# Three more feed-forward steps with P-Q+N on VectorE, and one batch load moved by two steps

## The chip, the core and the metric

The kernel runs on one core of a Trainium2 chip. The core has TensorE (matmuls into PSUM, an accumulator memory), VectorE, ScalarE and GpSimd (elementwise work; GpSimd also issues DMAs) and SyncE (issues DMAs). The engines run side by side, each through its own instructions in order, and wait for each other at semaphores. The metric is device time in microseconds (us); every time below is in that unit unless it says ns. In the profile's lines PE is TensorE, PEld its weight load, DVE VectorE, ACT ScalarE, POOL GpSimd, SP SyncE; L872 is line 872 of the kernel before.

## What is computed

```python
def _attn_ref(x):                      # x: (8, 3008, 256)
    X = np.fft.fft(x, axis=1)
    X = np.fft.fft(X, axis=2)
    return X.real.astype(np.float32)

def _moe_ref(x, w_in, w_out):          # (24064, 256), (256, 2048), (2048, 256)
    h = np.maximum(x @ w_in, 0.0)
    return (h * h @ w_out).astype(np.float32)
```

The second function is applied to the rows of the first one's result. So: the real part of a two-dimensional Fourier transform of each of eight batches, then a feed-forward layer with a squared ReLU, in float16 products with float32 sums.

## The kernel before, in words

*Columns and blocks.* The real part of the transform of real data is symmetric, so the kernel computes only half of its frequencies, 1505 columns per batch, 12040 in all. They are cut into 25 blocks, numbered from 0 (`w` in the loop over `range(NW)`); the widths are 240, 512, 376, 376, 512, 448, then 512, and the last one 360. For each column it holds two vectors, `zc` (cosine part) and `zs` (sine part). The first feed-forward product of a column is P+Q, with P from `zc` and Q from `zs`; that of its mirror frequency is P-Q. One row of `zs` (the Nyquist row) must not change its sign in the mirror image; N is the term that mends it.

*Steps.* The 2048 hidden units are taken in eight steps of 256 (`s` from 0 to 7, `NST` is 8). A step fills one of two PSUM buffers `ph` (two chunks of 128 units) and makes both results from it:

- A plain step: `pq` multiplies for P+Q (L859, L860, two each), ScalarE takes the ReLU (L891), `turn` adds -2Q to the same PSUM (L882, two matmuls), ScalarE takes the ReLU again (L891). VectorE squares both in one instruction, the power (L898).
- A VectorE step, one listed in `diff[w]`: `cosines` multiplies for P alone (L868, two), VectorE forms 2P+N from it (`twice`, L872, PSUM and SBUF to SBUF), `sines` adds Q to the PSUM (L877, two matmuls, which must wait for L872), ScalarE takes the ReLU of P+Q (L891), and VectorE adds 2P+N to the negated P+Q and clips (L889, the custom operation), which gives the ReLU of P-Q+N. ScalarE squares the first half (`power_act`, L902), VectorE the second (L898, half as long). There is no L882. N for the step is a product `n2` of the spread Nyquist row `zn` and the weights, two GpSimd instructions (L818) into one of three buffers.

Between the matmuls of a step stand one eighth of the second feed-forward product of the block before (`f2s`, L704, 128x256 each, its results leave through L719 on ScalarE and L683 on SyncE's queue), and, in some steps, a share of the matmuls that make the next block's `zc` and `zs` (`zl`, L581). `lo` and `hi` are the steps from which and before which these are dealt out. Their results leave PSUM by L586 and L592 on ScalarE and, for mirrored columns, by L610 on VectorE; when the next step is a VectorE step, `held` keeps L610 back until `settle` of that step, after its L872 and the power of the step before. In the step `hi` the Nyquist row of the next block starts its way (`spread_nyq`: L809 on ScalarE's queue to DRAM, L810 on GpSimd's queue back into all partitions); `nyq_rows` then makes the next block's n in the steps that follow, and what is left of them in step 0 of that block.

When two VectorE steps follow each other, the L889 of the first (`pend`) is put behind the L872 of the second, and one group of four L704 of the next step (`f2s[s].pop(0)()`) is done ahead of that step's first matmul.

*Batches.* A batch is loaded by three DMAs on GpSimd's queue (`load_x`: L127 and two L132), into the one buffer `xo`, and folded by VectorE in steps that `put` and `late` place: for each batch there is a block `b0`, with the first folds (L431, L442) in `b0 - 1`, more (L435, L445, L460, L448) in `b0`, the late folds (L488, L499, in steps 3, 4 and 5) in `b0 + 1`. `b0` is 5, 8, 10, 13, 16 and 19 for the batches 2 to 7 in order; batch 4, whose `b0` is two after the one before, is the one that is `tight`. A block in `shared` has its step 4's second power on ScalarE (L902) in step 5 instead of on VectorE.

What is listed in `diff` before: (4, 6) in blocks 3 to 5, (1, 3, 5, 7) in 6 and 7, (1, 3) in 9, (1, 2, 4, 6, 7) in 11, and so on. The order of the work on each engine is the order in which the Python code records it; nothing reorders it.

Of the kernel before, what the change touches and what calls it, by code (L numbers as in the profile page):

```python
# [29 lines left out]
def kernel(  # L30
# [15 lines left out]
    B, S, D = x.shape  # L46
# [33 lines left out]
    NW = len(wins)  # L80

    def win_of(col):
        return max(w for w in range(NW) if wins[w][0] <= col) if col < TOT else NW
# [5 lines left out]
    col_of = {}  # L89
# [60 lines left out]
    def load_rows(i):  # L150

        b, t = bs[i], xs[i]
        o = b * S * D
        if b == 0:
            nc.gpsimd.dma_start(out=t[0:1, 0, R - 1, :], in_=bass.AP(tensor=x.tensor, offset=x.offset + o, ap=[[D, 1], [1, D]]))
        if b + 1 == B:
            nc.gpsimd.dma_start(
                out=t[1:2, 2, :, :].rearrange("p c d -> p (c d)"),
                in_=bass.AP(tensor=x.tensor, offset=x.offset + o + (S - R) * D, ap=[[XW, 1], [1, XW]]))
# [578 lines left out]
    def fold_jobs(i):  # L738
        f = folds[i] = fold_steps(i)
        return [f["d_even"], f["n_cos"], lambda: (f["d_odd"](), f["load"]()), f["n_sin"], f["odds"], f["nyq"], lambda: (f["even"](), f["away"]()), f["back"]]  # L740

    NST = NFC // 2
    at_of = {w: [[] for _ in range(NST)] for w in range(NW)}
    post_of = {w: [[] for _ in range(NST)] for w in range(NW)}
    diff = {w: (4, 6) if w < 6 else (1, 3, 5, 7) if w < NW - 4 else (1, 2, 4, 6, 7) for w in range(3, NW)}
    backs = []
    shared = []

    def put(w, s, i, name, *k, d=at_of):
        d[w][s].append(lambda: folds[i][name](*k))  # L750

    def late(w, s, i, *st):
        at_of[w][s].append(lambda: run(*[folds[i]["late"][k] for k in st]))

    def make(i):
        folds[i] = fold_steps(i)

    for i in range(2, B):
        b0 = (win_of(col_of[i, 0]) + win_of(col_of[i - 1, 1])) // 2 - 1
        tight = b0 - 2 in [(win_of(col_of[j, 0]) + win_of(col_of[j - 1, 1])) // 2 - 1 for j in range(2, i)]  # L760
        near = i == 2 or tight
        at_of[b0 - 1][0].append(lambda i=i: make(i))
        at_of[b0 - 2][7].append(lambda i=i: load_rows(i))
        backs.append(b0)
        late(b0 + 1, 3, i, 0)
        late(b0 + 1, 4, i, 1)
        for k in (2, 3, 4):
            late(b0 + 1, 5, i, k)
        put(b0 - 1, 5 if near else 3, i, "d_even", 0)
        put(b0 - 1, (6 if tight else 7) if near else 5, i, "d_even", 1)  # L770
        put(b0 if i == 2 else b0 - 1, 0 if i == 2 else 7 if near else 6, i, "n_cos")
        put(b0, 0, i, "d_odd", 0)
        put(b0, 1, i, "d_odd", 1)
        put(b0, 2, i, "n_sin")
        put(b0, 3, i, "even")
        put(b0, 4, i, "away")
        put(b0, 5, i, "odds")
        put(b0, 6, i, "back")
        put(b0, 6, i, "nyq", d=post_of)
        if i + 1 < B and b0 > 5 and (win_of(col_of[i + 1, 0]) + win_of(col_of[i, 1])) // 2 - 1 > b0 + 2:  # L780
            put(b0 + 1, 2, i, "load")
        else:
            put(b0, 7, i, "load")
        if b0 > 5:
            diff[b0] = (2, 4, 6)
            diff[b0 + 1] = (1, 2, 4, 6, 7)
            shared.append(b0 + 1)
        if tight:
            diff[b0 - 1] = (1, 3)
            shared.remove(b0 - 1)  # L790
    n2s = {}
    BIG = 3.0e38
# [28 lines left out]
    for w in range(NW):  # L821
# [4 lines left out]
        lo, hi = 0, NST - 4 if 1 in diff.get(w + 1, ()) else NST - 3 if w + 1 in diff else NST - 2  # L826
        at, post = at_of[w], post_of[w]
        if w == 1:
            fj = fold_jobs(1)
            at = [[], fj[0:1], fj[1:2], fj[2:3], fj[3:5], [], [], []]  # L830
            post[5] = fj[5:6]
        elif w == 2:
            te = table_steps(1)
            at = [[folds[1]["even"], folds[1]["away"]], [lambda: te["freq"](), lambda: te["args"](0)], [lambda: f0s["v_part"](0)], [lambda: f0s["v_part"](1), f0s["even"], f0s["away"], f0s["back"]],
                  [lambda: te["turns"](0)], [lambda: te["mods"](0)], [lambda: te["absm"](0), lambda: te["sins"](0)], [lambda: te["coss"](0)]]
        elif w == 3:
            at[0] = [lambda: te["weigh"]()]
            for st in range(5):
                at[1 + st // 3] = at[1 + st // 3] + f0s["late"][st : st + 1]
            at[3] = [folds[1]["back"]]  # L840
            lo, hi = 3, NST - 1
        elif w == win_of(col_of[1, 1]) - 1:
            for st in range(5):
                at[min(st, 3)] += folds[1]["late"][st : st + 1]
            lo, hi = 4, NST - 1
# [217 lines left out]
```

## Time and profile before

| | |
|---|---|
| runs | 598.60, 597.36, 598.44; median 598.44 |
| the profiled execution | 597.31, of which the span from the first to the last instruction is 595.5 |
| granted TensorE clock, mean | 0.999 |
| TensorE busy | 584.9 (98% of the span), 4421 matmuls |
| VectorE busy | 497.0 (83%), 582 instructions |
| ScalarE busy | 462.2 (78%), 617 instructions |
| GpSimd busy | 243.9 (41%), 304 instructions |
| DMA | 50.33 MB, 85 GB/s on the mean |

The busy times are unions: overlapping instructions of one engine count once. A matmul's length in the records reaches into the next one, since they are pipelined, so a busy TensorE can still lose time; what a matmul costs is read from the time between two starts. In a line of the timeline the first number is the start in us from the span's start, the second the length, then engine, line, operation, output and inputs, shapes and the number of instructions merged; in brackets, where there is one, the idle time of the engine before it and what ended it.

### The profile page before, as it was taken

The page shows a single profiled execution, that of the slowest core. Times are in us where ns is not written, and L with a number is a line of the kernel's source. Part 1 is how long each engine was busy: PE and PEld are TensorE (multiplying, and loading weights), DVE is VectorE, ACT ScalarE, POOL GpSimd, SP SyncE. Part 2 cuts the span into 40 slices and gives each one's busy share as a digit, 9 for nine tenths or more (in the row PEclk, how much of TensorE's full clock was granted, in tenths as well). Part 3 has the DMA queues.
Part 4 walks back from the last instruction along what each step waited for, and adds up shares of the span by engine and source line. Part 5 has one row for each costly group of instructions (what it writes and reads, how often), then busy time and mean ns, then how long its engine had stood idle before and what let it go on. Part 6 is the DMA issues. An engine that isn't in the chain of part 4 may idle for free.

```text
span 595.5 us, 11299 instructions
## 1 busy us (share of the span) xinstructions
PE 584.9 (98%) x4421; PEld 424.9 (71%) x4421; DVE 497.0 (83%) x582; ACT 462.2 (78%) x617; POOL 243.9 (41%) x304
## 2 busy tenths in 40 slices
PE   7999999999999999999999999999999999999997
PEld 4567786776776777777777777777777777777786
DVE  8988686987989778979899799979899799888871
ACT  6796777967797787788878788877877788788762
POOL 8411423166514506183253651446505724425310
PEclk9999999999999999999999999999999999999999
DMA  8946421137211461246123442145312321211212
GB/s 149 154 87 149 123 73 44 48 108 148 61 44 55 129 138 49 72 101 155 41 59 108 94 116 58 38 121 115 90 39 90 87 58 37 61 47 48 61 56 70
DMA packets 37624, 50.33 MB, mean 85 GB/s; under 512 B 4589, under 2 KB 30755, under 8 KB 37571
## 3 DMA queue, kind: packets, MB, share of 16 engines
q0 software_dynamic: 10400, 24.94, 20.6%
q1 hardware_dynamic: 26899, 24.44, 13.6%
q8 instruction: 34, 0.56, 0.4%
q10 hardware_dynamic: 272, 0.23, 0.1%
q14 instruction: 19, 0.16, 0.1%
HBM read 36.42 MB, written 27.86 MB: 108 GB/s over the span
## 4 chain that ended last, share of the span: by engine, by line
PE 81%; DVE 10%; ACT 3%; POOL 2%; issue 2%; DMA 1%; DVEq 0%; ACTq 0%; POOLq 0%
PE po L704 47%; PE ph L882 6%; PE ph L859 6%; PE ph L860 6%; PE ph L877 6%; PE ph L868 5%; PE pz L581 4%; DVE h L898 2%; DVE t L872 2%; DVE h L889 2%; DMA xo<-in_x_dram,idx_r 1%; ACT h L891 1%; DVE zc L610 1%; ACT h L902 1%; POOL xo L132 1%
## 5 line engine op out<-in xcount | busy, mean ns | idle before, releaser
L704 PE MATMUL po<-wout,h 128*128 128x256 f16 (+1 forms) x3024 | 364.8, 273 | 0.0
L704 PEld LDWEIGHTS <-h 128*128 128x128 f16 (+1 forms) x3024 | 296.8, 98 | 75.1
L891 ACT ACTIVATE h<-ph 128x1024 f16<-128x1024 f32 (+3 forms) x301 | 287.6, 991 | 64.2 <-PE ph L877 41.1
L898 DVE TENSOR_TENSOR h<-h 128x2048 f16<-128x2048 f16 (+7 forms) x199 | 189.9, 960 | 22.1 <-ACT h L891 18.9
L818 POOL TENSOR_SCALAR n<-zn,g2n 128x512 f32<-128x512 f16 (+3 forms) x166 | 156.2, 954 | 68.7 <-DMA zn<-rd 55.5
L872 DVE SCALAR_TENSOR_TENSOR t<-ph,n 128x1024 f32<-128x1024 f32 (+3 forms) x83 | 99.1, 1194 | 37.5 <-PE ph L868 32.1
L889 DVE CUSTOM_DVE_ANT_0 h<-t,ph 128x1024 f16<-128x1024 f32 x74 | 90.0, 1216 | 15.5 <-ACT h L891 15.1
L902 ACT ACTIVATE h<-h 128x1024 f16<-128x1024 f16 (+3 forms) x87 | 90.3, 1038 | 0.5
L719 ACT ACTIVATE osb<-po 128x512 f32<-128x512 f32 (+3 forms) x95 | 55.0, 584 | 37.0 <-PE po L704 32.5
L859 PE MATMUL ph<-zc,gh 128*128 128x512 f16 (+3 forms) x218 | 80.3, 369 | 0.4 <-ACT h L950 0.3
L860 PE MATMUL ph<-zs,gh 128*128 128x512 f16 (+3 forms) x218 | 80.2, 368 | 0.0
L810 POOL DMA_DIRECT2D zn<-rd x22 | 12.7, 579 | 161.9 <-DMA rd<-zs 153.6
L882 PE MATMUL ph<-zs,gh 128*128 128x512 f16 (+3 forms) x218 | 62.5, 368 | 0.3 <-ACT h L891 0.3
L877 PE MATMUL ph<-zs,gh 128*128 128x512 f16 (+3 forms) x166 | 48.4, 373 | 0.9 <-DVE t L872 0.4
L868 PE MATMUL ph<-zc,gh 128*128 128x512 f16 (+3 forms) x166 | 48.4, 373 | 0.0
L859 PEld LDWEIGHTS <-gh 128*128 128x128 f16 x218 | 21.2, 97 | 22.9 <-DVE h L889 1.6
L860 PEld LDWEIGHTS <-gh 128*128 128x128 f16 x218 | 21.3, 98 | 22.1 <-issue 0.9
L868 PEld LDWEIGHTS <-gh 128*128 128x128 f16 x166 | 16.2, 98 | 18.9 <-issue 0.5
L882 PEld LDWEIGHTS <-gh 128*128 128x128 f16 x218 | 20.2, 98 | 4.1 <-issue 0.7
L586 ACT ACTIVATE es<-pz 128x376 f32<-128x376 f32 (+1 forms) x32 | 14.8, 485 | 8.9 <-PE pz L581 8.7
L464 POOL DMA_DIRECT2D scr<-ev x8 | 4.7, 582 | 40.7 <-DVE ev L460 34.8
L132 POOL DMA_INDIRECT xo<-in_x_dram,idx_r x15 | 17.7, 1182 | 4.5 <-issue 4.3
(143 smaller groups left out, 368.2 us busy)
## 6 DMA issues: line engine op xcount, KB each, us to landing
out_dram<-osb SPq DMA_DIRECT2D x77, 128.0 KB
xo<-in_x_dram POOLq DMA_DIRECT2D x7, 768.0 KB, 6.8
scr<-ev POOLq DMA_DIRECT2D x8, 390.0 KB, 4.0
zn<-rd POOLq DMA_DIRECT2D x19, 128.0 KB, 3.9
rb<-scr POOLq DMA_DIRECT2D x16, 130.0 KB, 3.9
out_dram<-osb SPq DMA_DIRECT2D x12, 94.0 KB
w<-in_moe_w_in_dram POOLq DMA_DIRECT2D x2, 512.0 KB, 10.0
wout<-in_moe_w_out_dram POOLq DMA_DIRECT2D x1, 1024.0 KB, 11.0
```

Of the source, the lines that this page charges most:

```text
L704: nc.tensor.matmul(po[0:m, j * D : (j + 1) * D], h2[:, fc, q : q + m], wout16[:, fc, :], start=(fc == 0 and not both), stop=(fc == NFC - 1 ...
L818: nc.gpsimd.tensor_scalar(out=n2[:, a, 0:wn1], in0=zns[wt][:, 0:wn1], scalar1=g2n[:, fc : fc + 1], scalar2=1.0, op0=ALU.mult, op1=ALU.mult)
L859: nc.tensor.matmul(ph[:, a, 0:wn], gh[:, 0, f0 : f0 + P], zcw[:, 0:wn], start=True, stop=False)
L860: nc.tensor.matmul(ph[:, a, 0:wn], gh[:, 1, f0 : f0 + P], zsw[:, 0:wn], start=False, stop=True)
L868: nc.tensor.matmul(ph[:, a, 0:wn], gh[:, 0, f0 : f0 + P], zcw[:, 0:wn], start=True, stop=True)
L872: nc.vector.scalar_tensor_tensor(out=t2[:, :, 0:wn], in0=phs[s][:, :, 0:wn], scalar=-2.0, in1=n2s[w, s][:, :, 0:wn], op0=ALU.mult, op1=ALU ...
L877: nc.tensor.matmul(phs[s][:, a, 0:wn], gh[:, 1, f0 : f0 + P], zsw[:, 0:wn], start=False, stop=True, skip_group_check=True)
L882: nc.tensor.matmul(phs[s][:, a, 0:wn], gh[:, 2, f0 : f0 + P], zsw[:, 0:wn], start=False, stop=True, skip_group_check=True)
L889: nc.vector._custom_dve(TENSOR_ADD_SAT, out=h, in0=t2s[s][:, :, 0:wn], in1=phs[s][:, :, 0:wn], s0=BIG, s1=0.0)
L891: nc.scalar.activation(h, phs[s][:, :, 0:wn], AF.Relu, bias=0.0, scale=-1.0)
L898: nc.vector.tensor_tensor(h, h, h, op=ALU.mult)
L902: nc.scalar.activation(h, h, AF.Square, bias=0.0, scale=1.0)
```

## The change

```diff
@@ -742,9 +742,9 @@
-    diff = {w: (4, 6) if w < 6 else (1, 3, 5, 7) if w < NW - 4 else (1, 2, 4, 6, 7) for w in range(3, NW)}
+    diff = {w: (4, 6, 7) if w == 3 else (4, 6) if w < 6 else (1, 3, 5, 7) if 6 < w < NW - 4 else (1, 2, 4, 6, 7) for w in range(3, NW)}
     backs = []
-    shared = []
+    shared = [6]
@@ -777,7 +777,7 @@
-        if i + 1 < B and b0 > 5 and (win_of(col_of[i + 1, 0]) + win_of(col_of[i, 1])) // 2 - 1 > b0 + 2:
+        if i + 1 < B and (win_of(col_of[i + 1, 0]) + win_of(col_of[i, 1])) // 2 - 1 > b0 + 2:
             put(b0 + 1, 2, i, "load")
         else:
             put(b0, 7, i, "load")
@@ -786,7 +786,7 @@
         if tight:
-            diff[b0 - 1] = (1, 3)
+            diff[b0 - 1] = (1, 2, 4)
             shared.remove(b0 - 1)
@@ -838,7 +838,7 @@
             at[3] = [folds[1]["back"]]
-            lo, hi = 3, NST - 1
+            lo, hi = 3, NST - 2
         elif w == win_of(col_of[1, 1]) - 1:
```

In block 3 step 7 becomes a VectorE step, the matmuls for block 4's `zc` and `zs` are dealt to steps 3 to 5 instead of 3 to 6, and the Nyquist row of block 4 starts in step 6 instead of 7. In block 6 the VectorE steps 1, 3, 5, 7 become 1, 2, 4, 6, 7, and the second power of step 4 goes to ScalarE. In block 9 they go from 1, 3 to 1, 2, 4. The load of batch 3's data moves from step 7 of block 5 to step 2 of block 6. Everywhere else the order of instructions stays as it was.

In all that is three VectorE steps more: six L882 less on TensorE, three L872, three L889 and some halved powers on VectorE, three pairs of L818 more on GpSimd, one L902 more on ScalarE for step 4 of block 6 (in the new VectorE steps an L902 stands for the second L891). In blocks 3 and 6 the steps 6 and 7 now follow each other, in blocks 6 and 9 the steps 1 and 2, with the changed order of L889 and L704 that goes with it.

## The prediction

> **What bounds the kernel now.** I read the busy time by stretches first, one stretch per block (from its first L859 or L868 to the next block's). Columns: stretch, its length, then busy time and instructions of TensorE, weight loads, VectorE, ScalarE, GpSimd, then granted clock, DMA share and rate.
> ```profile
> 70.90:89.56 18.66, 18.66 (x162) 15.07 (x160) 14.67 (x26) 14.52 (x23) 5.77 (x8) 1.00 0.26 74
> 134.14:157.41 23.27, 23.11 (x166) 16.02 (x164) 18.75 (x25) 17.92 (x24) 12.60 (x17) 1.00 0.57 122
> 204.87:230.25 25.38, 25.38 (x185) 18.00 (x184) 19.17 (x26) 19.88 (x28) 6.66 (x9) 1.00 0.51 110
> 254.75:279.32 24.57, 24.57 (x184) 17.71 (x182) 19.97 (x26) 20.10 (x29) 13.37 (x17) 1.00 0.57 131
> ```
> These are blocks 3, 6, 9 and, for comparison, 11, which already has the five steps that block 6 gets. TensorE is busy nearly throughout, VectorE for 75 to 81%: a step costs its matmuls, plus waits. Second, the timeline, for the price of a step (start, length, what):
> ```profile
> 154.80 0.59 PE L868 MATMUL ph<-zc,gh 128*128 128x512 f16 x2
> 155.23 1.91 PE L704 MATMUL po<-wout,h 128*128 128x256 f16 x16
> 155.50 1.23 DVE L872 SCALAR_TENSOR_TENSOR t<-ph,n 128x1024 f32<-128x1024 f32 x1
> 156.98 0.59 PE L877 MATMUL ph<-zs,gh 128*128 128x512 f16 x2
> ...
> 180.03 1.22 DVE L872 SCALAR_TENSOR_TENSOR t<-ph,n 128x1024 f32<-128x1024 f32 x1
> 181.30 0.59 PE L877 MATMUL ph<-zs,gh 128*128 128x512 f16 x2 [0.38 <-DVE t L872]
> ```
> Two 512-column matmuls take 0.43 (154.80 to 155.23), sixteen L704 take 1.75, so twelve take 1.31. L872 starts 0.70 after L868, and L877 can start 1.27 after L872 (180.03 to 181.30, where it waited). So a VectorE step needs 0.70+1.27 = 1.97 between L868 and L877; TensorE gives 2.18 with sixteen L704 between them, only 1.74 with twelve. Summing what start-to-start times exceed these spacings: 0 in blocks 3 and 9, 0.48 in 6 (step 5: 0.18 before L868, 0.30 before L877), 0.55 in 7, 1.05 in 4. Third, the end of block 3:
> ```profile
> 85.06 0.48 PE L868 MATMUL ph<-zc,gh 128*128 128x376 f16 x2
> 85.38 1.47 PE L704 MATMUL po<-wout,h 128*128 128x256 f16 x12
> 85.43 0.83 ACT L891 ACTIVATE h<-ph 128x752 f16<-128x752 f32 x1
> 85.66 0.94 DVE L872 SCALAR_TENSOR_TENSOR t<-ph,n 128x752 f32<-128x752 f32 x1 [0.42 <-PE ph L868]
> 86.51 0.93 DVE L898 TENSOR_TENSOR h<-h 128x1504 f16<-128x1504 f16 x1
> 87.45 0.62 DVE L610 SCALAR_TENSOR_TENSOR zs<-es,pz 128x135 f16<-128x135 f32 x2
> 87.98 0.61 DVE L610 SCALAR_TENSOR_TENSOR zc<-es,pz 128x135 f16<-128x135 f32 x2
> 88.51 0.94 DVE L889 CUSTOM_DVE_ANT_1 h<-t,ph 128x752 f16<-128x752 f32 x1
> 89.56 0.38 PE L859 MATMUL ph<-zc,gh 128*128 128x512 f16 x1
> 92.08 0.59 PE L882 MATMUL ph<-zs,gh 128*128 128x512 f16 x2 [0.18 <-ACT h L891]
> ```
> Step 6: VectorE does L872, the power of step 5, four L610, then L889. Block 4's first L882 waits for ScalarE.
>
> **The change, part by part.**
>
> *Matmuls removed.* Three steps lose two L882 each: 2 x 0.43 (blocks 6, 9) + 0.32 (376 columns, 85.06 to 85.38) = 1.18 off.
>
> *Block 3: +1.16.* The z matmuls go from 5,5,5,5 in steps 3 to 6 to 6,7,7,0, so step 6's L868 starts 0.29 later (the time of its z, 86.69 to 86.98): 85.35, and L872 at 85.95. The power of step 5 needs that step's second L891 on ScalarE, and the two L592 copies now stand before it: L719 moves from 84.95 to 85.15, copies from 85.63, 0.38 each, L891 from 86.39 to 87.21. Power at 87.26, 0.94 to the next start; four L610, 0.53 a pair, to 89.26. Only there stands L872 of the new step 7: it ends at 90.20, L877 goes at 90.25. TensorE was ready at 85.35 + 0.32 + 1.31 + 0.32 + 0.32 + 1.31 = 88.93: a wait of 1.32. Queued behind it are four L704 and block 4. After 0.32 and 0.44 it is 91.01; L859 needs the PSUM of step 6, which L889 reads after L872 (89.26 + 0.85, + 0.94 = 91.05): 91.10. Only eight L704 are left to stand between this product and its L882, 0.87, so L882 waits for ScalarE: L891 starts 1.07 after L859 where ScalarE is free (block 12: 279.32 and 280.39), takes 1.02, L882 comes 0.05 later: 93.24, against 92.08. The same work is then done, so +1.16, with the 0.32 saved and block 4's old wait of 0.35 already in it. On ScalarE L809 now waits for the zs L610 (88.7); behind it are L902 and step 7's L891, not due before 90.8. Bounds: had VectorE no delay, 88.93 + 0.32 + 0.44 + 2.14 = 91.83, -0.25; with the longest power row of the trace (1.74 for 1.22) +1.7. I take 1.16, since each row has its twin in the fence.
>
> *Block 6: -0.40.* Its 112 L704 are dealt 12, 16, 12, 16 ...; its VectorE steps were those with sixteen. Now steps 2, 4, 6 have twelve. Step 2 has three z (0.48) as cover, 4 and 6 nothing: 0.23 each. Entering block 7, L859 waits 0.05 for L889, as block 12 does after 11. The old 0.48 goes (step 5 is no VectorE step now): -0.43 - 0.48 + 0.51. VectorE gets 2.44 (L872, L889), loses 0.53 (half of a power) and 0.69 (step 4's half goes to ScalarE, L902 1.06, hidden: ScalarE has 17.9 of 23.3): 20.0 of 22.9. By TensorE's spacings steps 1 to 4 start 3.08, 6.17, 9.26 and 12.35 after the block does. From step 4's L872 (13.05) on I find no gap over 0.12 on VectorE: to the next start 1.14, power 1.14, L610 0.52, L488 0.61, L889 1.26, two L499 0.74 (18.46); L872 of step 6 (L868 at 17.80, so 18.50) 1.14, power 1.14, L872 of step 7 (20.90) 1.14, and L889 of step 6 from 22.04 to 23.25, for which block 7's L859 waits. Bounds: -0.91 (no wait) to +0.3 (a wait like block 7's 0.55 at one step more, and 0.15).
>
> *Block 9: -0.43.* Steps 0 to 4 are like block 11's, which wait nowhere over 0.03. Step 4 starts at 217.61, its L872 at 218.31; with 1.14, 1.14, 0.52, 0.61, 0.52 before it and 1.22 of its own, its L889 ends at 223.46. Step 6's L859 needs that PSUM at 223.74: cover 0.23 beyond the 0.05 of a semaphore. If a power is 0.52 longer, 0.29 is lost: -0.43 to -0.14.
>
> *Load of the next batch.* L127 and two L132 (0.78, 1.02, 0.95) leave GpSimd at 136.44 to 139.80 and go behind the n of step 7, whose buffer comes free with step 2's L872 (6.17 + 0.70 + 1.23 = 8.10 into block 6, 142.2; n of step 6 waits likewise for step 1's): about 143.7 to 147. They land 7.2 to 8.4 later, by 155.4, and are needed at 168 (L428, L431): no cost; uncovered, each us late would be one on the path. Behind them on GpSimd stand zn for block 7 and L505/L506. zn landed 7.3 after L809 in block 6, but 9.1, 8.4 and 10.1 in blocks 11, 14, 17, where such a load runs beside it. With L809 at 149.1: 157.5 to 159.2, plus 1.4 for two L818; block 7's first L872 needs them at 161.0 and has 0.45 to spare: 0, at worst 0.3.
>
> *GpSimd.* Six more L818, 0.69 each, in its idle 59%. They can hold VectorE: the 2048-element L898 takes 1.216 alone (52 rows), 1.322 beside L818 (26 rows, longest 1.736), L872 1.22 in both. [...] By the rows a pair costs 0.1, mostly beside slack: 0.
>
> Sum: 1.16 - 0.40 - 0.43 = +0.33. The profiled execution, 597.31 (595.5 span and 1.8 around it), becomes 597.6. The median of the runs shown is 598.44, 1.1 above it, so 598.8 is the time to expect.
>
> **Rivals.** *A, TensorE alone decides.* Block 3's wait does not form: -0.25 there, -0.91 and -0.43: -1.59, 596.85. For it: 98% busy, every removed matmul counts. Against: rows at 86.51 to 88.51, where VectorE is in order and L872 must follow. *B, VectorE is held in its run without gaps in block 6.* From 13.05 to 23.25 each us on VectorE is one for TensorE. Two whole powers and a half one in or just behind it, at the longest (0.52, 0.52, 0.50), add 1.54: 0.33 + 1.54 = +1.87, 600.3; it decides from 0.87 up. For it: the rows beside L818 above. Against: L818 for block 7 waits for zn until about 24 into the block. [...] *C, block 3 comes out even* (its wait as long as what it saves): -0.83, inside 0.2%. That the change might not do what it says is out: its program has three L872 and three L889 more and six L882 less, at the steps named.
>
> **Numbers.** Within 0.2% (1.2 us, about what a measurement of this kernel can tell from no change): forecast 0.55 and C 0.05, 0.60. A 0.14, faster. B and anything else that lengthens that run or block 3's, slower, 0.26. The forecast's own range is -0.7 to +1.2: 597.7 to 599.6. For 8 in 10 it is widened by most of A and B: 597.1 to 600.3.
>
> **What would show it.** Block 3 to block 4's first L882 1.2 later than 92.08, with L877 of step 7 named as waiting for t of L872 (right); less than 0.4 later would break the largest term. Waits of about 0.23 before L877 in steps 4 and 6 of block 6, none in 2; block 9 at 24.95; xo landed before 156; no wait for n at block 7's step 1. If a block beyond 10 differs in length, I missed a link.

## The result, and the profile after

| | before | changed |
|---|---|---|
| median of 11 runs each | 597.72 (597.33 to 598.66) | 599.35 (598.42 to 600.06) |
| ratio to before, 95% interval | | 1.0021 (1.0012 to 1.003) |
| the profiled execution, its span | 597.31, 595.5 | 599.24, 597.5 |
| from the first matmul of block 1 to the end | 566.88 | 567.80 |
| TensorE busy, matmuls | 584.9, 4421 | 585.3, 4415 |

The changed kernel is slower by about 0.2%, so the interval lies on both sides of the bound that the prediction set for "no change". Not all of the 1.63 between the medians is the change's. The runs of each kernel fall into two groups about 1 us apart, whichever kernel it is: those with a mean granted clock of 0.998 or more, and those with 0.997 or less, in whose profiles the start is longer (last section); and the 11 runs of the changed kernel caught the longer start more often. Counted from the first matmul of block 1, which leaves the start out, the change costs 0.92. Runs of one group say the same: of the runs at a mean clock of 0.998 or more, the 47 of before that ran beside the experiments (a single slow one, of 1245.5, is left out) have a mean of 597.45, the four of the changed kernel 598.61, 1.16 more.

The stretches of blocks 3, 6, 9 and 14 in the changed kernel, with the same columns as before (stretch, length, busy time and instructions of TensorE, weight loads, VectorE, ScalarE and GpSimd, clock, DMA share and rate); block 3 starts 0.95 later than before, because of that start:

```profile
71.85:91.75 19.90, 19.04 (x165) 15.15 (x162) 15.93 (x27) 15.26 (x25) 9.16 (x11) 1.00 0.25 73
135.95:159.28 23.33, 23.18 (x167) 16.05 (x166) 19.88 (x26) 19.73 (x26) 13.27 (x16) 1.00 0.55 116
206.32:231.64 25.32, 25.11 (x184) 17.81 (x183) 20.97 (x28) 19.93 (x28) 8.59 (x11) 1.00 0.52 110
327.61:352.56 24.95, 24.85 (x184) 17.70 (x182) 20.28 (x26) 20.48 (x29) 13.16 (x17) 1.00 0.56 119
```

Block 3 is 1.24 longer than before (18.66), and block 4 gives 0.37 of that back. Block 9 should have lost 0.43 and lost 0.06. Block 14, whose work the change doesn't touch, went from 24.57 to 24.94. TensorE's idle time in these rows (0.86, 0.15, 0.21 and 0.10) is less than its waits, since part of a wait hides in the modelled length of the matmul before it (a pair of L868 is 0.59 long in the profile and takes 0.43 from start to start); the waits below are read from start to start.

The end of block 3 in the timeline:

```profile
87.15 0.83 ACT L891 ACTIVATE h<-ph 128x752 f16<-128x752 f32 x1
88.02 0.94 DVE L898 TENSOR_TENSOR h<-h 128x1504 f16<-128x1504 f16 x1 [0.18 <-ACT h L891]
88.87 0.61 DVE L610 SCALAR_TENSOR_TENSOR zs<-es,pz 128x135 f16<-128x135 f32 x2
89.39 0.61 DVE L610 SCALAR_TENSOR_TENSOR zc<-es,pz 128x135 f16<-128x135 f32 x2
89.92 0.93 DVE L872 SCALAR_TENSOR_TENSOR t<-ph,n 128x752 f32<-128x752 f32 x1
90.90 0.48 PE L877 MATMUL ph<-zs,gh 128*128 128x376 f16 x2 [0.86 <-DVE t L872]
93.90 0.59 PE L882 MATMUL ph<-zs,gh 128*128 128x512 f16 x2 [0.24 <-ACT h L891]
```

This is the queue that the prediction named: the power of step 5 waits for ScalarE, four L610 follow, then L872 of step 7, and L877 waits for it. By spacings of starts the wait is 1.03, then 0.10 before block 4's first L859 and 0.40 before its first L882.

Steps 4 and 6 of block 6:

```profile
149.03 1.23 DVE L872 SCALAR_TENSOR_TENSOR t<-ph,n 128x1024 f32<-128x1024 f32 x1
150.30 0.59 PE L877 MATMUL ph<-zs,gh 128*128 128x512 f16 x2
...
155.75 0.59 PE L877 MATMUL ph<-zs,gh 128*128 128x512 f16 x2
```

Both L877 start 0.24 later than the matmuls before them allow: twelve L704 are too short a cover for the 1.97 of L868 to L877. The other wait of the block is 0.05 on entering block 7.

### The profile page after: what moved, and what is told of

The parts are those of the page before. It is cut to its first block, busy times and chain, and to the rows that moved or that the text cites. A ratio compares the mean times of both kernels' runs of the same rounds, so it can differ in the third digit from the quotient of the medians.

```text
span 597.5 us, 11302 instructions
## 1 busy us (share of the span) xinstructions
PE 585.3 (98%) x4415; PEld 424.1 (71%) x4415; DVE 499.4 (84%) x586; ACT 464.3 (78%) x618; POOL 251.4 (42%) x310
## 3 DMA queue, kind: packets, MB, share of 16 engines
q0 software_dynamic: 10400, 24.94, 20.8%
## 4 chain that ended last, share of the span: by engine, by line
PE 82%; DVE 8%; ACT 5%; POOL 2%; issue 2%; ACTq 0%; DVEq 0%; POOLq 0%
PE po L704 46%; PE ph L882 6%; PE ph L859 6%; PE ph L860 6%; PE ph L877 6%; PE ph L868 5%; PE pz L581 4%; DVE t L872 3%; ACT h L891 2%; DVE h L898 2%; DVE h L889 2%; ACT h L902 1%; PE pg L527 1%; DVE zs L610 1%; DVE zc L610 1%
## 5 line engine op out<-in xcount | busy, mean ns | idle before, releaser
L704 PE MATMUL po<-wout,h 128*128 128x256 f16 (+1 forms) x3024 | 365.4, 273 | 0.0
L704 PEld LDWEIGHTS <-h 128*128 128x128 f16 (+1 forms) x3024 | 296.8, 98 | 75.9
L891 ACT ACTIVATE h<-ph 128x1024 f16<-128x1024 f32 (+3 forms) x298 | 285.5, 991 | 63.7 <-PE ph L877 39.6
L898 DVE TENSOR_TENSOR h<-h 128x1024 f16<-128x1024 f16 (+6 forms) x197 | 186.0, 950 | 21.6 <-ACT h L891 16.8
L818 POOL TENSOR_SCALAR n<-zn,g2n 128x512 f32<-128x512 f16 (+3 forms) x172 | 162.0, 956 | 70.4 <-DMA zn<-rd 51.2
L872 DVE SCALAR_TENSOR_TENSOR t<-ph,n 128x1024 f32<-128x1024 f32 (+3 forms) x86 | 102.5, 1192 | 39.6 <-PE ph L868 32.1
L889 DVE CUSTOM_DVE_ANT_0 h<-t,ph 128x1024 f16<-128x1024 f32 x76 | 92.4, 1216 | 12.5 <-ACT h L891 11.2
L902 ACT ACTIVATE h<-h 128x1024 f16<-128x1024 f16 (+3 forms) x91 | 94.2, 1035 | 0.9 <-ACT h L891 0.3
L719 ACT ACTIVATE osb<-po 128x512 f32<-128x512 f32 (+3 forms) x95 | 54.9, 583 | 35.8 <-PE po L704 30.8
L859 PE MATMUL ph<-zc,gh 128*128 128x512 f16 (+3 forms) x212 | 78.2, 369 | 0.5 <-ACT h L950 0.3
L860 PE MATMUL ph<-zs,gh 128*128 128x512 f16 (+3 forms) x212 | 78.1, 369 | 0.0
L882 PE MATMUL ph<-zs,gh 128*128 128x512 f16 (+3 forms) x212 | 60.8, 368 | 0.6 <-ACT h L891 0.6
L877 PE MATMUL ph<-zs,gh 128*128 128x512 f16 (+3 forms) x172 | 50.0, 372 | 1.7 <-DVE t L872 1.2
L868 PE MATMUL ph<-zc,gh 128*128 128x512 f16 (+3 forms) x172 | 50.1, 373 | 0.0
L859 PEld LDWEIGHTS <-gh 128*128 128x128 f16 x212 | 20.6, 97 | 22.7 <-DVE h L889 2.1
L860 PEld LDWEIGHTS <-gh 128*128 128x128 f16 x212 | 20.7, 98 | 21.1 <-issue 0.9
L868 PEld LDWEIGHTS <-gh 128*128 128x128 f16 x172 | 16.8, 98 | 19.4 <-issue 0.2
L882 PEld LDWEIGHTS <-gh 128*128 128x128 f16 x212 | 19.7, 98 | 4.3 <-issue 1.1
L877 PEld LDWEIGHTS <-gh 128*128 128x128 f16 x172 | 16.1, 97 | 6.3 <-issue 2.9
```

Of the source, the lines that this page charges most:

```text
L704: nc.tensor.matmul(po[0:m, j * D : (j + 1) * D], h2[:, fc, q : q + m], wout16[:, fc, :], start=(fc == 0 and not both), stop=(fc == NFC - 1 ...
L818: nc.gpsimd.tensor_scalar(out=n2[:, a, 0:wn1], in0=zns[wt][:, 0:wn1], scalar1=g2n[:, fc : fc + 1], scalar2=1.0, op0=ALU.mult, op1=ALU.mult)
L859: nc.tensor.matmul(ph[:, a, 0:wn], gh[:, 0, f0 : f0 + P], zcw[:, 0:wn], start=True, stop=False)
L860: nc.tensor.matmul(ph[:, a, 0:wn], gh[:, 1, f0 : f0 + P], zsw[:, 0:wn], start=False, stop=True)
L868: nc.tensor.matmul(ph[:, a, 0:wn], gh[:, 0, f0 : f0 + P], zcw[:, 0:wn], start=True, stop=True)
L872: nc.vector.scalar_tensor_tensor(out=t2[:, :, 0:wn], in0=phs[s][:, :, 0:wn], scalar=-2.0, in1=n2s[w, s][:, :, 0:wn], op0=ALU.mult, op1=ALU ...
```

## The experiments

The lengths below are from the first L859 or L868 of a block to that of the next; the sum is from the first matmul of block 1 to the end. The times are means of the runs at a mean clock of 0.998 or more (three to seven for each experiment), since the medians depend on how many runs of each group a kernel caught; ratio and interval are those of all runs. Two things limit these columns. Block 1, whose own work no edit touches, is 20.46 to 20.74 long in these profiles, so a sum is good to about 0.1; the columns by block are the finer measure. And the experiments ran on three chips, on which the mean of before is 597.53 (e1, e3, e6, e7), 597.38 (e2, e4, e5, e8) and 597.47 (e9 to e12).

| | blocks 3+4 | 6+7 | 9+10 | 14 | sum | time | ratio |
|---|---|---|---|---|---|---|---|
| before | 40.89 | 47.60 | 49.87 | 24.57 | 566.88 | 597.45 | |
| changed | 41.76 | 47.23 | 49.94 | 24.94 | 567.80 | 598.61 | 1.0021 (1.0012 to 1.003) |
| e1 | 40.89 | 47.24 | 49.82 | 24.57 | 566.70 | 597.08 | 0.9994 (0.9984 to 1.0003) |
| e2 | 41.76 | 47.63 | 49.88 | 24.57 | 567.92 | 598.20 | 1.0015 (1.0004 to 1.0025) |
| e3 | 40.69 | 47.29 | 49.94 | 24.94 | 566.70 | 597.22 | 1.0001 (0.9991 to 1.001) |
| e4 | 40.89 | 47.23 | 49.88 | 24.57 | 566.48 | 597.04 | 0.9994 (0.9984 to 1.0003) |
| e5 | 40.89 | 47.77 | 49.88 | 24.57 | 567.00 | 597.51 | 1.0009 (0.9999 to 1.0018) |
| e6 | 40.89 | 47.60 | 49.82 | 24.57 | 566.84 | 597.33 | 1.0 (0.9991 to 1.001) |
| e7 | 40.88 | 47.61 | 49.45 | 24.57 | 566.32 | 596.89 | 0.9993 (0.9983 to 1.0002) |
| e8 | 41.76 | 47.26 | 49.95 | 24.94 | 567.68 | 598.34 | 1.0016 (1.0006 to 1.0025) |
| e9 | 40.89 | 47.61 | 49.45 | 24.57 | 566.59 | 596.72 | 0.9986 (0.9976 to 0.9995) |
| e10 | 40.69 | 47.42 | 49.57 | 24.94 | 566.55 | 596.94 | 0.9991 (0.9982 to 1.0001) |
| e11 | 41.76 | 47.23 | 49.82 | 24.57 | 567.25 | 597.97 | 1.001 (1.0001 to 1.002) |
| e12 | 40.70 | 47.29 | 49.45 | 24.57 | 566.03 | 596.41 | 0.9983 (0.9974 to 0.9992) |

### Block 3: is it that edit, and is it the order on VectorE? (e1, e2, e3)

e1 is the changed kernel with block 3 as before:

```diff
-    diff = {w: (4, 6, 7) if w == 3 else (4, 6) if w < 6 else (1, 3, 5, 7) if 6 < w < NW - 4 else (1, 2, 4, 6, 7) for w in range(3, NW)}
+    diff = {w: (4, 6) if w < 6 else (1, 3, 5, 7) if 6 < w < NW - 4 else (1, 2, 4, 6, 7) for w in range(3, NW)}
@@ ... @@
-            lo, hi = 3, NST - 2
+            lo, hi = 3, NST - 1
```

> The changed kernel with block 3 as before (steps 4 and 6, z in steps 3 to 6). Theory: the whole loss lies in block 3's pair and its wake, so the stretch from block 3's first L859 to block 5's is back at 40.89 (after: 41.76), and everything behind stays as in the changed kernel: 6 and 7 together 47.23, 9 and 10 together 49.94. Time 0.9 below the changed kernel, within 0.1 of the kernel before. Rival (each of the three steps costs about a third of the loss): 0.3 below the changed kernel. Block 14's extra 0.37 goes away if it hangs on how many instructions VectorE has had before, and stays if it hangs on the moved load.

e2 is the kernel before with these two lines of the change alone.

> The kernel before with block 3's part of the change alone. Theory: blocks 3 and 4 together 41.76 (before: 40.89), all later blocks as before, time 0.9 above the kernel before. Rival (thirds): 0.3 above. Block 14 keeps 24.57 unless its extra 0.37 hangs on this edit.

e3 is the changed kernel with the z matmuls dealt to steps 3 and 4 alone, so that the four L610 stand before the L889 of step 4:

```diff
-            lo, hi = 3, NST - 2
+            lo, hi = 3, NST - 3
```

> The changed kernel with block 3's z dealt to steps 3 and 4 alone (10 and 10), so that the four L610 stand before L889 of step 4 and no longer between the power of step 5 and L872 of step 7. Theory (the order on VectorE makes the wait): the 1.03 before L877 of step 7 falls to 0.1 or less; L872 of step 7 starts 0.70 after its L868; blocks 3 and 4 together 40.8 (from L877 on: 0.32, four L704 0.44, L859, then 2.14 to L882), 0.9 to 1.0 less than in the changed kernel. Rival (VectorE is simply too slow for two such steps on 376 columns, wherever L610 stands): the wait stays above 0.6 and blocks 3 and 4 together above 41.4.

e1 and e2 put the whole of +0.87 on block 3's edit: 40.89 without it, 41.76 with it alone. (Of what their sums hold beyond that, 0.16 and 0.15 are a wait of L877 in step 1 of block 18, where L872 waits for n; the same wait is 0.10 in e12. It isn't there in the changed kernel.) e3 takes the wait of block 3 away. VectorE there, and the L877 of step 7:

```profile
83.67 0.61 DVE L610 SCALAR_TENSOR_TENSOR zc<-es,pz 128x135 f16<-128x135 f32 x2
84.20 0.94 DVE L889 CUSTOM_DVE_ANT_1 h<-t,ph 128x752 f16<-128x752 f32 x1
...
86.78 0.94 DVE L898 TENSOR_TENSOR h<-h 128x1504 f16<-128x1504 f16 x1
87.79 0.94 DVE L872 SCALAR_TENSOR_TENSOR t<-ph,n 128x752 f32<-128x752 f32 x1
88.83 0.48 PE L877 MATMUL ph<-zs,gh 128*128 128x376 f16 x2
```

With the L610 done before step 5 has ended, L872 of step 7 follows the power at once, L877 has no wait, and blocks 3 and 4 take 40.69, 0.20 less than before. So the order made the wait, not the number of instructions. Nearly all of it is the order on VectorE: from the first L610 to L872 the changed kernel spends 1.05. The edit of e3 also moves the two L592 copies out of ScalarE's way, and with them goes the 0.18 that the power waited for ScalarE; the two were not tried one by one. The 0.40 before block 4's first L882 stays, as only eight L704 stand ahead of it there as well.

### Block 6: the edit alone, without its load, and with its products dealt otherwise (e4, e5, e8)

e4 is the kernel before with block 6's parts alone (its five steps, its place in `shared`, the load).

> The kernel before with block 6's part alone: steps 1, 2, 4, 6, 7, the half power of step 4 on ScalarE, the load in step 2. Theory: blocks 6 and 7 together 47.23 (before: 47.59), waits of 0.24 before L877 in steps 4 and 6 and none at step 5; time 0.36 below the kernel before. Rival (the pairs cost as in block 3): 47.6 or more.

e5 is e4 with the load left where it was, in step 7 of block 5:

```diff
-        if i + 1 < B and (win_of(col_of[i + 1, 0]) + win_of(col_of[i, 1])) // 2 - 1 > b0 + 2:
+        if i + 1 < B and b0 > 5 and (win_of(col_of[i + 1, 0]) + win_of(col_of[i, 1])) // 2 - 1 > b0 + 2:
```

> As the run with block 6 alone, but the load stays in step 7 of block 5. Theory (the load is covered in both places): blocks 6 and 7 together within 0.05 of the run with the load moved, xo landing some 8 earlier. Rival (the load in its old place makes the n of block 6 late on GpSimd, or in the new one makes zn late): a difference of 0.3 or more, seen as a wait of L872 for n in block 6 or in step 1 of block 7.

e8 is the changed kernel with block 6's L704 dealt 12, 16, 12, 12, 16, 12, 16, 16 (an entry of the list is four), so that steps 4 and 6 have sixteen:

```diff
-        f2s = [list(spread(f2, s, NST)) for s in range(NST)]
+        f2s = [list(spread(f2, s, NST)) for s in range(NST)] if w != 6 else [list(f2[a:b]) for a, b in ((0, 3), (3, 7), (7, 10), (10, 13), (13, 17), (17, 20), (20, 24), (24, 28))]
```

> The changed kernel with block 6's 112 L704 dealt 12, 16, 12, 12, 16, 12, 16, 16 to the eight steps, so that the VectorE steps 4 and 6 have sixteen. Theory (from step 4 on VectorE has no gap, and its run ends the block): the waits of 0.24 before L877 in steps 4 and 6 shrink to 0.16 and 0, but step 6's L868 then waits about 0.37 for L889 of step 4, and from block 6's first L859 to block 7's is 23.33 as before this edit, within 0.1. Rival (only the number of L704 in the two steps counts): both waits gone, 22.85, time 0.48 below the changed kernel.

e4 gave what the theory says, 47.23 and the waits of 0.24, 0.24 and 0.05. e5 was a miss for it: the load's move is not free, it is worth 0.54 (47.77 against 47.23). GpSimd, VectorE and TensorE in steps 1 and 2 of e5:

```profile
139.78 6.11 POOL L818 TENSOR_SCALAR n<-zn,g2n 128x512 f32<-128x512 f16 x8
140.24 0.59 PE L868 MATMUL ph<-zc,gh 128*128 128x512 f16 x2
141.48 1.22 DVE L872 SCALAR_TENSOR_TENSOR t<-ph,n 128x1024 f32<-128x1024 f32 x1 [1.27 <-POOL n L818]
```

The load keeps GpSimd until 139.78, and step 2's n comes behind it: L872 starts 1.24 after its L868 instead of 0.70. L877 loses 0.30, the next L859 0.27. Step 2 is one of the three steps that are new on VectorE, and only the moved load lets GpSimd have its n in time. The move has a price as well, in block 7's zn; it is told with the mends below.

e8 did what its theory says. The wait in step 4 shrank from 0.24 to 0.15 and that in step 6 went, but L868 of step 6 now waits 0.34 for the L889 of step 4, and block 6 was 23.36 long instead of 23.33. TensorE, with a shorter wait and four L704 less on its way, comes to step 6 sooner, only to wait for VectorE there. So cover won for TensorE alone brings nothing, and the rival, 22.85, falls.

### Block 9: where the expected 0.43 stayed (e6, e7)

ScalarE in steps 5 and 6 of block 9, first where L428 stands in the kernel before, then the changed kernel:

```profile
221.33 1.94 ACT L891 ACTIVATE h<-ph 128x1024 f16<-128x1024 f32 x2
223.15 0.40 ACT L428 ACTIVATE xo<-xo 1x256 f16<-1x256 f16 x1
```

```profile
224.16 1.06 ACT L902 ACTIVATE h<-h 128x1024 f16<-128x1024 f16 x1
225.11 0.40 ACT L428 ACTIVATE xo<-xo 1x256 f16<-1x256 f16 x1
...
225.69 0.59 ACT L719 ACTIVATE osb<-po 128x512 f32<-128x512 f32 x1
226.18 1.93 ACT L891 ACTIVATE h<-ph 128x1024 f16<-128x1024 f32 x2
228.16 0.59 PE L882 MATMUL ph<-zs,gh 128*128 128x512 f16 x2 [0.21 <-ACT h L891]
```

In the changed kernel an L902, which a VectorE step needs and a plain step doesn't, stands in step 5 ahead of the two L428 of the next batch, of L719 and of the two L891 that steps 5 and 6 wait for; the L882 of step 6 comes 0.375 late. Before, L428 came straight behind the L891, the two L891 behind it ended at 226.37, and L882 followed at 226.78 without a wait. ScalarE has no more work than before (19.88 and 19.93 in the block, 28 instructions in both), since this L902 stands for the second L891 of step 4; but it stands a step later than that one did. e6 is the kernel before with block 9's edit alone; e7 is e6 with that L902 left until step 6:

```diff
         def first(s):
             relu(s, 0)
-            run(*plus)
-            plus.clear()
+            if (w, s) == (9, 5): return
+            run(*plus); plus.clear()
```

> The kernel before with block 9's steps 1, 2, 4 alone. Theory: L902 of step 4 now stands on ScalarE before the two L428 and L719 of step 5, so that step 6's L882 waits about 0.37 for its L891 and blocks 9 and 10 together stay within 0.15 of the 49.87 of before, though 0.43 of matmuls is gone. Rival (that wait came from the changes in blocks 3 and 6, by a late load or a shifted queue): no wait in block 9, blocks 9 and 10 together 49.44. The 0.15 before L877 in step 4 of block 10 and the 0.37 in block 14 show up if they belong to this edit.

> As the run with block 9's steps alone, but L902 of step 4 runs in step 6, behind that step's first L891, instead of in step 5. Theory (ScalarE's order makes the wait): L882 of step 6 waits no more, blocks 9 and 10 together 49.45 to 49.6, time 0.3 to 0.4 below the kernel before. Rival (ScalarE has too little room in the block, so the wait comes back at the next L882): the sum of waits in blocks 9 and 10 stays at 0.37 over that of before and their length at 49.85.

e6 has the wait, so it is this edit's. In e7 it is gone, and blocks 9 and 10 take 49.45, 0.42 less than before:

```profile
223.83 1.94 ACT L891 ACTIVATE h<-ph 128x1024 f16<-128x1024 f32 x2
225.64 1.07 ACT L902 ACTIVATE h<-h 128x1024 f16<-128x1024 f16 x1
226.18 0.59 PE L882 MATMUL ph<-zs,gh 128*128 128x512 f16 x2
```

The two L891 now go ahead of L902, and L882 follows at TensorE's own pace.

### Block 14, which nobody touched (e11)

Of the first eight experiments, block 14 is 24.94 long in just those that have all three edits (e3, e8), as in the changed kernel. There, in step 7:

```profile
349.09 0.59 PE L868 MATMUL ph<-zc,gh 128*128 128x512 f16 x2
350.14 1.23 DVE L872 SCALAR_TENSOR_TENSOR t<-ph,n 128x1024 f32<-128x1024 f32 x1 [0.61 <-POOL spn L506]
351.42 0.59 PE L877 MATMUL ph<-zs,gh 128*128 128x512 f16 x2
```

L872 starts 1.05 after L868 where 0.70 is enough. The L506 in the bracket ended at 349.73, and L872 started 0.41 after that. In program order the row ahead of L872 is the semaphore wait that belongs to it. Counted with such rows, this L872 is number 447 of VectorE (the first is 0); the L872 of block 10 that holds up L877 by 0.15 is number 319, and one in block 6 that delays nobody is 191: 128 apart, each starting 0.40 to 0.43 after its wait's row has ended instead of 0.04. The same three rows are late by as much in e3, e8 and e10. In e2, with block 3's edit alone, row 191 is an L872 as well and starts 0.42 after its wait's row, while rows 319 and 447 are something else and block 14 keeps its 24.57. e11 is the changed kernel with one more instruction at the start of VectorE's program:

```diff
-    nc.vector.memset(halfpi, float(math.pi / 2))
+    nc.vector.memset(halfpi, float(math.pi / 2)); nc.vector.memset(small([P, 1], "pad1"), 0.0)
```

> The changed kernel with one more tiny VectorE instruction at its start (a memset of 128x1 that nobody reads, on line 187). In the changed kernel the VectorE rows number 191, 319 and 447 of the trace, 128 apart, are each an L872 that starts 0.30 to 0.42 us after the end of its own semaphore row instead of 0.04, in blocks 6, 10 and 14. Theory, VectorE's instructions come in pieces of 128 and a piece that begins between a wait and its instruction makes the instruction late: one instruction more moves the boundary, the three L872 follow their semaphore by 0.04 to 0.06, block 14 is 24.57 us instead of 24.94, the 0.15 before L877 of step 4 in block 10 is gone, and from the first matmul of block 1 to the end it is 567.3 instead of 567.80. Rival, the stall comes from the work itself (traffic or GpSimd at that place): block 14 stays at 24.94.

The same place in e11:

```profile
347.90 0.59 PE L868 MATMUL ph<-zc,gh 128*128 128x512 f16 x2
348.59 1.23 DVE L872 SCALAR_TENSOR_TENSOR t<-ph,n 128x1024 f32<-128x1024 f32 x1 [0.24 <-POOL spn L506]
350.08 0.59 PE L877 MATMUL ph<-zs,gh 128*128 128x512 f16 x2
```

L872 is 0.69 behind L868 again, and only the 0.24 for L506 is left of its wait. All three late instructions are gone, block 14 is 24.57 long, block 10 loses its extra wait, and the sum falls by 0.55, 0.48 of it in these two blocks, with the work of the blocks unchanged. The rival, traffic or GpSimd at that place, falls.

### Both mends together (e9, e10, e12)

e9 has blocks 6 and 9 changed, block 3 as before, and the L902 of e7. e10 is the changed kernel with the edits of e3 and e7. e12 is e10 with the one instruction of e11.

> Blocks 6 and 9 changed, block 3 as before, L902 of step 4 of block 9 run in step 6. Theory: blocks 3 and 4 40.89 us as before, blocks 6 and 7 47.23, blocks 9 and 10 49.45, block 14 24.57; from the first matmul of block 1 to the end 566.1 against 566.88, ratio 0.9987. Rival, a stall of VectorE lands in another block: one block of 13 to 24 longer by 0.15 to 0.4, 566.3 to 566.5.

> All three edits with both mends: block 3's z matmuls in steps 3 and 4 (so that the four L610 stand before the L889 of step 4), and L902 of step 4 of block 9 run in step 6. Theory: the mends add up. Blocks 3 and 4 together 40.7 us (before 40.89), blocks 6 and 7 47.25 (47.60), blocks 9 and 10 49.5 to 49.6 (49.87), block 14 24.94 (24.57) since VectorE's late L872 there comes with this number of VectorE instructions; from the first matmul of block 1 to the end 566.2 against 566.88, ratio about 0.999. Rival, the two mends spoil each other or block 9's wait comes back elsewhere: 566.7 or more.

> Both mends and the one tiny VectorE instruction. Theory: as the kernel with both mends, without the late L872: block 14 24.57 us, blocks 9 and 10 49.45, from the first matmul of block 1 to the end 565.7 against 566.88 before, ratio about 0.998. Rival, the boundary falls on another wait that matters: one other block longer by 0.15 to 0.4.

The blocks that were mended came out as expected: 40.69 and 40.70 in e10 and e12, 49.45 in e9 and e12, 49.57 in e10, block 14 at 24.94 in e10 and 24.57 in the others. The sums are 0.3 to 0.5 above the expectation. In e10 and e12 about 0.2 of that is an error in adding up: the block lengths expected there make 566.4 and 565.9, not 566.2 and 565.7. In e9 0.10 is block 1. The rest is for the most part a wait that wasn't in it: L877 of step 1 of block 7 waits 0.37 in e9, 0.19 in e10, 0.06 in e12 (0 in the changed kernel, 0.06 in e3), as L872 there waits for n, and n for zn.

The moved load has a part in that. In the five kernels with the load in its old place (before, e2, e5, e6, e7) the first of these L818 starts 21.78 to 22.08 into block 6, in the nine with the load moved 25.30 to 26.12. e4 and e5, which differ in the load alone, have 25.72 and 22.08. So zn comes 3.6 later when the load is issued shortly ahead of it, which uses up nearly all the room that the L872 has, and small differences then decide: the L818 starts at 25.30 in the changed kernel, 25.50 in e12, 25.81 in e9 and 26.12 in e10, and in e9, where the wait is longest, the first L818 takes 1.19 beside an L898 of VectorE, against 0.69 in e10. A place for the load that spares both block 6's n and zn was not tried.

e12 is the best of the kernels: ratio 0.9983 (0.9974 to 0.9992), sum 0.85 and time 1.04 below before. The whole interval lies below 1, as that of e9 does.

## Why the prediction came out as it did

The forecast was +0.33, and 598.8. The median is 599.35, inside its range and inside the forecast's own (597.7 to 599.6), but the sum was right only in part:

| term | predicted | measured |
|---|---|---|
| block 3 with block 4 | +1.16 | +0.87 |
| block 6 with block 7 | -0.40 | -0.37 |
| block 9 | -0.43 | -0.06 |
| the load's move, GpSimd | 0 | 0 seen |
| blocks 10 and 14 | not there | +0.13 and +0.37 |
| sum | +0.33 | +0.94 |

All other blocks and the end make -0.02, which gives the 0.92 of the whole. That the time lies inside the range is in part luck: two terms and the two blocks that were not thought of erred on one side (0.37 in block 9, 0.03 in block 6, 0.50 in blocks 10 and 14), block 3 on the other (0.29), and the base of 598.44 was too high. Counted from the 597.72 of the 11 runs, the forecast would have been 598.05, and the medians differ by 1.63, more than the 1.2 that the range allowed. The step from the profiled execution to the median (1.1, taken over from the three runs of before) was in fact the two groups of starts: 597.36 was a short one, 598.44 and 598.60 are near the mean of the long ones.

*Block 3: right mechanism, sized 0.29 too long.* All places named were met: the wait before L877, 0.10 before L859 (0.09 said) and 0.40 before L882 (0.41 by its sum); the first was 1.03 long, not 1.32. With the 0.95 of the start taken off, L872 of step 7 is at 88.97 (89.26 said), L877 at 89.95 (90.25) and L882 at 92.95 (93.24). Two rows explain the 0.29. The power was put at 0.94 to the next start, which is its length; from start to start it is 0.85 (88.02 to 88.87). And the chain on ScalarE ahead of it ended at 87.03 with the same 0.95 taken off, not at 87.21, since L719 had not been put off as far as was said (84.99, not 85.15). Rival C (block 3 comes out even) and rival A (no wait) both fall.

*Block 6: right in sum and in places.* The waits are 0.24, 0.24 and 0.05 against 0.23, 0.23 and 0.05, none in step 2. The run of VectorE starts 13.08 into the block (13.05 said), and its last L889 ends at 23.27 (23.25); there is one gap in it of 0.15, before L872 of step 6 (none over 0.12 was said). No power in it was held: both took 1.22. So rival B, VectorE held up in this run, didn't occur. Nor was it put to the test: the run lasts from 149.03 to 159.22, and in the changed kernel's profile no L818 starts after 144.81 and before 161.25. By the prediction's rows of before, a power beside an L818 is 0.1 longer on the mean and 0.52 at most (1.322 and 1.736 against 1.216).

*The load: the sum right, the reason in part wrong.* "They land 7.2 to 8.4 later, by 155.4" does not hold. The changed kernel's profile doesn't tell the landing, but those of e1 and e3 do, with the same load in the same place: 11.0 to 13.4 after the issue, the last at 159.5 and 158.8. So the sign "xo landed before 156" was missed. It cost nothing: the first reader of xo starts at 167.6 and 167.4 there, at 169.4 in the changed kernel, and nobody waited for xo. What the text didn't see is that leaving the load in its place would have cost 0.54 (e5). That zn would come late beside the load it did see; its bound for that, "0, at worst 0.3", met 0 in the changed kernel and 0.37 at the worst in e9.

*Block 9: the step that failed.* "Steps 0 to 4 are like block 11's, which wait nowhere over 0.03" and then the cover of 0.23 for the L889 of step 4. That cover did hold: no L859 waits there. But in a VectorE step an L902 on ScalarE takes the place of the second L891 and stands a step later; in block 9, not in 11, this L902 meets the L428 of the next batch. The text had counted L902 for block 6 ("1.06, hidden"), and for block 9 it had read VectorE only, the engine that the edit is named for. The L882 of step 6 waits 0.375, and -0.06 is outside the -0.43 to -0.14 that the text gave. The two errors, 0.29 and 0.37, all but cancel.

*The missed link.* "If a block beyond 10 differs in length, I missed a link": block 14 did. The link is no wait in the program but the number of VectorE instructions ahead of it. Without it, e11 gives +0.37 against the forecast of +0.33; that they are so near is chance, by the two errors that cancel and by a block 1 that is 0.15 shorter in e11's profile than in before's.

## What to carry to other kernels

Where an operation is moved from one engine to another, list every engine that the new form uses and read each one's queue at that place, the one with plenty of idle time too: here an L902 of 1.06, a step later on ScalarE than the L891 that it replaces, took back 0.37 of the 0.43 that TensorE had won. When an added step makes a product late, look first at the order on the engine that makes it: four small instructions, dealt two steps earlier, turned a wait of 1.03 into none. And when a block that was not edited changes its length, shift the program by one idle instruction before looking for a cause in the data flow: here that brought block 14 from 24.94 back to 24.57.

## What was not expected of the hardware

*Three L872 of VectorE, 128 rows apart, start late.* In the changed kernel the L872 in rows 191, 319 and 447 start 0.40 to 0.43 after their wait's row has ended instead of 0.04, so they are late by 0.35 to 0.38. In e11, with one row more ahead of them, none is late. That the place of one instruction in the count decides it is shown; that the program comes in pieces of 128, as the theory of e11 has it, is not, and neither is what the late L872 waits for. The profile's DMA queues have one of the kind "instruction" with 19 transfers of 8,192 bytes in the span, and in the changed kernel one of these starts 0.7 to 1.6 after each of the three late L872 (at 140.80, 246.56 and 351.71), so only after it has begun. Whose instructions they are the profile doesn't say.

*The start takes 1 us more in about half of the runs.* One group of early matmuls in the profiled execution of the changed kernel, and below it the same group in e11, which had the short start:

```profile
16.62 1.12 PE L581 MATMUL pz<-cos,od 128*128 128x376 f16 x3
```

```profile
16.63 0.65 PE L581 MATMUL pz<-cos,od 128*128 128x376 f16 x3 [0.56 <-ACT od L407]
```

Three matmuls of one shape take 1.12 in the one and 0.65 in the other, from the same start on, and the first matmul of block 1 comes at 29.67 instead of 28.68; the mean clock is 0.996 against 0.999. In the changed kernel's profile the granted clock is one half from 15.27 to 18.68; in e11's there is no such stretch in the start. Of the 14 profiles the six with a long start (changed, e2, e4, e8, e9, e10) have one there, 3.41 long in each, and the other eight have none. Of the 94 runs of before beside the experiments 47 have 0.998 or more and a mean of 597.45, 47 have less and a mean of 598.42. What decides whether a run has the stretch, no run shows. For a change worth less than 1 us, compare within a group, or from a matmul behind the start.
